# Retention and channel mix on one core: key scaling, key loads, the decay table and the first blocks put in another order

## The chip, the core and the metric

The kernel runs on one core of a Trainium2 chip. TensorE (PE) multiplies matrices, VectorE (DVE) and ScalarE (ACT) work on elements and read TensorE's results from PSUM, GpSimd (POOL) works on elements in SBUF and issues some of the loads, SyncE (SP) issues the others and the stores. Each engine runs its instructions in the order in which they are written; semaphores make one wait for another. The metric is the device time of one execution in microseconds.

## What is computed

A retention layer (linear attention with a decay for each head) whose output goes through a channel mix:

```python
for t in range(S):                                   # B=4, H=8, S=768, D=64
    state = gamma * state + einsum('bhd,bhe->bhde', k[:, :, t], v[:, :, t])
    y[:, :, t] = scale * einsum('bhd,bhde->bhe', q[:, :, t], state)
x = y.transpose(0, 2, 1, 3).reshape(B, S, 512)
x_prev = x shifted by one token, 0 at the start
xk = mu_k * x + (1 - mu_k) * x_prev;  xr = mu_r * x + (1 - mu_r) * x_prev
k = max(xk @ w_k, 0)                                 # 512 -> 1024
out = sigmoid(xr @ w_r) * (k * k @ w_v)              # 1024 -> 512
```

## The kernel before

The 768 tokens of a batch are cut into 6 chunks of 128, so there are 24 chunks (`c`); two chunks make a block of 256 tokens (`m`, 12 of them) for the channel mix.

For a chunk, `load` brings keys as float32 on SP's queue and q and v as float16 on GpSimd's queue. `kscale` (line 108) multiplies the keys by a decay table `gk` and gives `ks`, on GpSimd. `transposes` has TensorE turn q and `ks` (`pT`), and ScalarE copy them (`qkT`). `scores` makes `pA`, masked by VectorE to `a2t`. `state` adds keys times values to the state (`pS`), scaled by VectorE to `sbd`. `retained` makes `pY` from the state and the scores, and VectorE multiplies it by the decay table `gy` into `xT` (line 174).

For a block, `shift` takes the difference `dx` of neighbouring tokens on GpSimd (line 183) and makes four `xk` and four `xr` from it on VectorE (line 188). `keys` is four groups of 8 matmuls (`pZ`), each squared by ScalarE in two operations (`kr`, `k`). `gate` (`pR`, `rsb`) and `values` (`pV`, 8 matmuls for each half) follow a block later, and `store` multiplies them on VectorE (`osb`, line 232) and writes them out.

The order is written by hand. In the loop over `m`, with `a = 2 * (m + 1)`, the scores, states and retained outputs of chunks `a` and `a + 1` alternate with the key groups of block `m`. Then come `shift(m + 1)` and `ahead(a + 2)`, which scales and transposes one chunk, a gate, `ahead(a + 3)`, a gate, and the values of block `m - 1`. So on GpSimd the scaling of a chunk stands behind `dx`, and on TensorE its transposes follow at once. All loaded tiles have five buffers, and the loads of two chunks are written at the top of each turn. `gy` (128 x 512 float32) is loaded from memory.

```python
    ld = pool("ld", 5)
    att = pool("att", 4)
    psa = pool("psa", 4, space=PS)
    psm = pool("psm", 4, space=PS)
```

Of the kernel before, what the change touches and what calls it, by code (L numbers as in the profile page):

```python
# [18 lines left out]
def kernel(  # L19
# [239 lines left out]
    def ahead(c):  # L259
        if c < NC:  # L260
            kscale(c)
            transposes(c)
# [12 lines left out]
    shift(0)
    ahead(2)
    ahead(3)
    for m in range(NBLK + 1):
        a = 2 * (m + 1)
        p = m - 1  # L280
        z = m < NBLK
        if p > 0:
            store(p - 1, 1)
        maybe(load, a + 2)
        maybe(load, a + 3)
        maybe(scores, a)
        maybe(state, a)
        if z:
            keys(m, 0)
        maybe(scores, a + 1)  # L290
# [14 lines left out]
        if p >= 0:
            gate(p, 1)
            values(p, 0)
            store(p, 0)
            values(p, 1)
# [31 lines left out]
```

## Time and profile before

| | us |
|---|---|
| median of 3 runs (227.29 to 228.06) | 227.64 |
| the profiled execution | 227.42 |
| its span, first to last instruction | 225.6 |
| TensorE busy in it (matmuls) | 169.7 |
| VectorE busy | 132.4 |
| ScalarE busy | 98.3 |
| GpSimd busy | 94.5 |

The rows that the prediction uses stand in a section below. In a row of the timeline the first number is the start, the second the time that the row's instructions took together, then come engine, line, operation, the tile written and the tiles read, and how many instructions the row joins; in brackets is how long the engine had been idle and what it waited for. [...] Matmuls are pipelined, so their durations overlap.

### The profile page before, as it was taken

The numbers are of one execution on the slowest core, as the hardware profiler recorded it, in microseconds if no ns is written. First come the engines' busy times: TensorE is split into PE (matmuls) and PEld (weight loads), VectorE is DVE, ScalarE is ACT, GpSimd is POOL, SyncE is SP. The second block draws the span as 40 slices with busy tenths as digits, with TensorE's granted clock in tenths as the row PEclk, the third lists the DMA queues.
The fourth block names the chain that finished last, engine by engine and source line by source line (L and its number), as shares of the span: only waits on it lengthen the run. The fifth ranks groups of instructions, "written<-read, shape, count | busy, mean of one in ns | idle before, by whom it ended". The sixth has DMA issues, their size and how long they took to land.

```text
span 225.6 us, 3597 instructions
## 1 busy us (share of the span) xinstructions
PE 169.7 (75%) x1444; PEld 106.8 (47%) x1444; DVE 132.4 (59%) x220; ACT 98.3 (44%) x146; POOL 94.5 (42%) x92
## 2 busy tenths in 40 slices
PE   0128495877869977986868977986878986999993
PEld 0015264564545564463544464563454464575641
DVE  0007694948747648558747648568748558467022
ACT  2012245566365265165265264166265164163920
POOL 8760845729048039029149029019139025002000
PEclk9999999699996996999996996999996996999999
DMA  7999999954926934943936943942934940100222
GB/s 94 189 194 165 175 198 161 65 35 26 197 62 41 162 79 29 162 93 21 194 67 40 154 88 25 153 100 18 183 82 34 157 92 3 66 27 3 93 93 93
DMA packets 82464, 22.06 MB, mean 98 GB/s; under 512 B 76560, under 2 KB 79248, under 8 KB 82448
## 3 DMA queue, kind: packets, MB, share of 16 engines
q0 software_dynamic: 52544, 8.92, 50.5%
q1 hardware_dynamic: 28848, 12.92, 23.6%
q8 instruction: 11, 0.18, 0.3%
q10 hardware_dynamic: 1056, 0.00, 0.2%
q14 instruction: 5, 0.04, 0.1%
HBM read 24.46 MB, written 6.29 MB: 136 GB/s over the span
## 4 chain that ended last, share of the span: by engine, by line
PE 53%; DVE 16%; issue 11%; POOL 11%; DMA 8%; POOLq 0%; DVEq 0%
PE pV L223 18%; PE pR L213 12%; PE pZ L200 10%; DMA v<-in_v_dram 8%; DVE a2t L132 5%; POOL ks L108 5%; PE pT L117 3%; PE pY L168 3%; DVE osb L232 3%; DVE xT L174 3%; DVE sbd L150 3%; POOL q L102 2%; PE pY L162 2%; PE pS L141 2%; POOL v L104 2%
## 5 line engine op out<-in xcount | busy, mean ns | idle before, releaser
L183 POOL TENSOR_TENSOR dx<-xT 128x1024 f32<-128x1024 f32 x12 | 22.7, 1888 | 106.1 <-DVE xT L174 106.1
L205 ACT ACTIVATE kr<-pZ 128x512 f32<-128x512 f32 x48 | 28.6, 596 | 65.1 <-PE pZ L200 64.9
L188 DVE SCALAR_TENSOR_TENSOR xk<-dx,muk,xT 128x256 f16<-128x256 f32 x48 | 37.1, 832 | 24.7 <-POOL dx L183 24.7
L200 PE MATMUL pZ<-xk,wk 128*128 128x256 f16 x384 | 51.0, 279 | 0.0
L119 ACT COPY qkT<-pT 128x1024 f16<-128x1024 f16 x24 | 24.3, 1013 | 44.2 <-PE pT L117 44.0
L223 PE MATMUL pV<-wv,k 128*128 128x512 f16 x192 | 43.4, 379 | 0.0
L132 DVE TENSOR_TENSOR a2t<-pA,c_sb 128x512 f16<-128x512 f32 x48 | 30.7, 680 | 16.8 <-PE pA L126 16.8
L200 PEld LDWEIGHTS <-wk 128*128 128x128 f16 x384 | 35.7, 100 | 6.2
L117 PE MATMUL pT<-c_sb,ks 128*128 128x128 f16 x96 | 12.5, 270 | 34.7 <-POOL ks L108 34.5
L232 DVE SCALAR_TENSOR_TENSOR osb<-pV,rsb 128x512 f32<-128x512 f32 x24 | 16.5, 691 | 34.8 <-PE pV L223 17.0
L206 ACT ACTIVATE k<-kr 128x512 f16<-128x512 f32 x48 | 30.2, 630 | 1.5
L213 PE MATMUL pR<-wr,xr 128*128 128x512 f16 x96 | 30.6, 456 | 0.0
L223 PEld LDWEIGHTS <-k 128*128 128x128 f16 x192 | 18.8, 98 | 22.7 <-issue 0.2
L108 POOL TENSOR_TENSOR ks<-k,csm_sb 128x512 f16<-128x512 f32 x24 | 26.4, 1119 | 0.1
L117 PEld LDWEIGHTS <-ks 128*128 128x128 f16 x96 | 7.9, 121 | 37.6 <-POOL ks L108 37.6
L174 DVE TENSOR_TENSOR xT<-pY,gy_sb 128x512 f32<-128x512 f32 x24 | 16.6, 691 | 12.9 <-PE pY L168 12.5
L102 POOL DMA_DIRECT2D q<-in_q_dram x24 | 22.3, 928 | 0.8 <-POOLq L325 0.8
L104 POOL DMA_DIRECT2D v<-in_v_dram x24 | 21.6, 898 | 0.4 <-DMA v<-in_v_dram 0.4
L188 DVE SCALAR_TENSOR_TENSOR xr<-dx,mur,xT 128x256 f16<-128x256 f32 x48 | 19.9, 473 | 0.0
L115 PE MATMUL pT<-c_sb,q 128*128 128x128 f16 x96 | 11.7, 258 | 9.9 <-DMA q<-in_q_dram 9.9
L218 ACT ACTIVATE rsb<-pR 128x512 f32<-128x512 f32 x24 | 14.3, 600 | 8.0 <-PE pR L213 7.9
L150 DVE TENSOR_TENSOR sbd<-pS,csm_sb 128x512 f16<-128x512 f32 x24 | 16.3, 680 | 0.0
(22 smaller groups left out, 101.1 us busy)
## 6 DMA issues: line engine op xcount, KB each, us to landing
k<-in_k_dram SPq DMA_DIRECT2D x24, 256.0 KB, 4.0
out_dram<-osb SPq DMA_DIRECT2D x24, 256.0 KB, 2.1
q<-in_q_dram POOLq DMA_DIRECT2D x24, 128.0 KB, 4.0
v<-in_v_dram POOLq DMA_DIRECT2D x24, 128.0 KB, 4.4
wk<-in_moe_w_k_dram POOLq DMA_DIRECT2D x2, 512.0 KB, 12.7
wv<-in_moe_w_v_dram POOLq DMA_DIRECT2D x1, 1024.0 KB, 23.9
wr<-in_moe_w_r_dram POOLq DMA_DIRECT2D x1, 512.0 KB, 19.1
gy_sb<-cgy SPq DMA_DIRECT2D x1, 256.0 KB, 5.4
```

The lines of the kernel that those rows point to most:

```text
L102: nc.gpsimd.dma_start(out=Q16[c], in_=q[b, :, t, :].rearrange("h t d -> t h d"))
L104: nc.gpsimd.dma_start(out=V16[c], in_=v[b, :, t, :].rearrange("h t d -> t h d"))
L108: nc.gpsimd.tensor_tensor(out=KS[c], in0=K32[c], in1=gk[:, :, None].to_broadcast([P, H, D]), op=ALU.mult)
L117: nc.tensor.transpose(pT[:, 1, j, :], KS[c][:, 2 * j : 2 * j + 2, :], ident)
L119: nc.scalar.copy(out=QKT[c], in_=pT)
L132: nc.vector.tensor_tensor(out=A2[c][:, hp], in0=pA[hp], in1=causal[:, None, :].to_broadcast([P, NJ, C]), op=ALU.mult,)
L188: nc.vector.scalar_tensor_tensor(out=dst[:, j], in0=dx[:, j], scalar=mu[:, j : j + 1], in1=xprev[:, j], op0=ALU.mult, op1=ALU.add,)
L200: nc.tensor.matmul(pZ[:, i, :], lhsT=wk16[:, co, fo * P : fo * P + P], rhs=XK[m][:, co, :], start=(i == 0 and co == 0), stop=(co == NCO - ...
L205: nc.scalar.activation(out=kr, in_=pZ, func=AF.Relu)
L206: nc.scalar.activation(out=K2[m][:, 2 * g : 2 * g + 2], in_=kr, func=AF.Square)
L213: nc.tensor.matmul(pR, lhsT=XR[m][:, co, tb * P : tb * P + P], rhs=wr16[:, co, :], start=(co == 0), stop=(co == NCO - 1),)
L223: nc.tensor.matmul(pV, lhsT=K2[m][:, fo, tb * P : tb * P + P], rhs=wv16[:, fo, :], start=(fo == 0), stop=(fo == NFO - 1),)
```

## The change

Five things are changed.

The scaling of keys (`kscale`) can be given an engine. Chunks 0 to 3 are scaled on VectorE, all others on GpSimd as before. In the loop the scaling of chunks `a + 2` and `a + 3` is written at the top of a turn, and their transposes stay at its end, behind `shift(m + 1)`.

Loads of keys are apart from loads of q and v. Keys have a pool of two buffers, and the load of chunk `c + 2` is written behind the scaling of chunk `c`; q and v have eight buffers and are loaded two chunks earlier than before.

The decay table `gy` isn't loaded. VectorE sets its first column and doubles the filled part seven times, with the powers `pw` that are added to the small table `csm`.

The first key load leads SP's queue, ahead of the small tables.

Blocks 0 and 1 are written out by hand: the four key groups of block 0 stand together behind `shift(0)`, and chunks 2 and 3 come after them; the keys of block 1 stand together behind `shift(1)`, followed by both gates of block 0, the transposes of 4 and 5, and the values of block 0 between their scores. The scaling and the transposes of 6 and 7 stand behind `shift(2)`. The loop then runs from `m = 2`.

```diff
-    ld = pool("ld", 5)
+    ld = pool("ld", 8)
+    ldk = pool("ldk", 2)
...
-    def kscale(c):
+    def kscale(c, eng=None):
         KS[c] = att.tile([P, H, D], F16, name="ks16")
-        nc.gpsimd.tensor_tensor(
+        (eng or nc.gpsimd).tensor_tensor(
             out=KS[c], in0=K32[c], in1=gk[:, :, None].to_broadcast([P, H, D]), op=ALU.mult
         )
...
+    loadk(0)
     nc.sync.dma_start(out=csm, in_=smalld.ap())
     nc.sync.dma_start(out=c16, in_=c16d.ap())
+    loadk(1)
...
-    nc.sync.dma_start(out=gy, in_=gyd.ap().rearrange("p (j t) -> p j t", j=NJ))
...
+    nc.vector.memset(gy[:, :, 0:1], 0.125 * KSC)
+    for l in range(LOG):
+        n = 1 << l
+        nc.vector.tensor_tensor(
+            out=gy[:, :, n : 2 * n], in0=gy[:, :, 0:n],
+            in1=pw[:, l, :, None].to_broadcast([P, NJ, n]), op=ALU.mult,
+        )
...
+    for c in (0, 1):
+        kscale(c, nc.vector)
+        loadk(c + 2)
+        transposes(c)
     for c in (0, 1):
         scores(c)
         state(c)
     retained(0)
     retained(1)
     shift(0)
-    ahead(2)
-    ahead(3)
+    for g in range(4):
+        keys(0, g)
+    for c in (2, 3):
+        kscale(c, nc.vector)
+        loadk(c + 2)
+        transposes(c)
...
+    shift(1)
+    kscale(4)
+    loadk(6)
+    kscale(5)
+    loadk(7)
+    for c in range(6, 10):
+        loadqv(c)
+    for g in range(4):
+        keys(1, g)
+    gate(0, 0)
+    gate(0, 1)
+    transposes(4)
+    transposes(5)
+    values(0, 0)
...
+    shift(2)
+    kscale(6)
+    loadk(8)
+    kscale(7)
+    loadk(9)
+    transposes(6)
+    transposes(7)
+    for m in range(2, NBLK + 1):
         a = 2 * (m + 1)
         p = m - 1
         z = m < NBLK
-        if p > 0:
-            store(p - 1, 1)
-        maybe(load, a + 2)
-        maybe(load, a + 3)
+        store(p - 1, 1)
+        for c in (a + 2, a + 3):
+            maybe(kscale, c)
+            maybe(loadk, c + 2)
+        maybe(loadqv, a + 4)
+        maybe(loadqv, a + 5)
...
         maybe(shift, m + 1, NBLK)
-        maybe(ahead, a + 2)
-        if p >= 0:
-            gate(p, 0)
-        maybe(ahead, a + 3)
...
+        maybe(transposes, a + 2)
+        gate(p, 0)
+        maybe(transposes, a + 3)
```

GpSimd around `dx` of block 3 and block 4, before; `ks_773` and `ks_793` are the keys of chunks 8 and 9, whose transposes TensorE has next:

```order
L183 TENSOR_TENSOR dx<-xT_88 128x1024
L108 TENSOR_TENSOR ks_773<-k_635,csm_sb 128x512
L108 TENSOR_TENSOR ks_793<-k_641,csm_sb 128x512
L102 DMA q_839<-in_q_dram 128x8x64
L104 DMA v_841<-in_v_dram 128x8x64
L102 DMA q_845<-in_q_dram 128x8x64
L104 DMA v_847<-in_v_dram 128x8x64
L183 TENSOR_TENSOR dx<-xT_88 128x1024
```

The same place of GpSimd now; `ks_859` and `ks_863` are the keys of chunks 10 and 11, whose transposes stand behind the second `dx` of these rows:

```order
L191 TENSOR_TENSOR dx<-xT_91 128x1024
L116 TENSOR_TENSOR ks_859<-k_659,csm_sb 128x512
L116 TENSOR_TENSOR ks_863<-k_663,csm_sb 128x512
L110 DMA q_867<-in_q_dram 128x8x64
L112 DMA v_869<-in_v_dram 128x8x64
L110 DMA q_871<-in_q_dram 128x8x64
L112 DMA v_873<-in_v_dram 128x8x64
L191 TENSOR_TENSOR dx<-xT_91 128x1024
```

The kinds of rows are the same; the scaling has moved ahead by two chunks.

VectorE at the start of the program, before:

```order
L248 MEMSET xT_87 128x4
L248 MEMSET xT_88 128x4
L248 MEMSET xT_89 128x4
L248 MEMSET xT_90 128x4
L132 TENSOR_TENSOR a2t<-pA_156,c_sb 128x512
L132 TENSOR_TENSOR a2t<-pA_157,c_sb 128x512
```

VectorE at the same place now:

```order
L268 MEMSET gy_sb 128x4
L271 TENSOR_TENSOR gy_sb<-gy_sb,csm_sb 128x4
L271 TENSOR_TENSOR gy_sb<-gy_sb,csm_sb 128x4x2
L271 TENSOR_TENSOR gy_sb<-gy_sb,csm_sb 128x4x4
L271 TENSOR_TENSOR gy_sb<-gy_sb,csm_sb 128x4x8
L271 TENSOR_TENSOR gy_sb<-gy_sb,csm_sb 128x4x16
L271 TENSOR_TENSOR gy_sb<-gy_sb,csm_sb 128x4x32
L271 TENSOR_TENSOR gy_sb<-gy_sb,csm_sb 128x4x64
L116 TENSOR_TENSOR ks_136<-k_96,csm_sb 128x512
L116 TENSOR_TENSOR ks_151<-k_100,csm_sb 128x512
L140 TENSOR_TENSOR a2t<-pA_166,c_sb 128x512
```

The table's eight instructions and two scalings now stand ahead of the first masking of scores.

ScalarE at the start, before; each `COPY` brings one chunk's transposes to SBUF:

```order
L119 COPY qkT<-pT 128x1024 x4
L205 ACTIVATE kr<-pZ 128x512
L206 ACTIVATE k_292<-kr 128x512
L205 ACTIVATE kr<-pZ 128x512
L206 ACTIVATE k_292<-kr 128x512
```

ScalarE at the same place now:

```order
L127 COPY qkT<-pT 128x1024 x2
L213 ACTIVATE kr<-pZ 128x512
L214 ACTIVATE k_243<-kr 128x512
L213 ACTIVATE kr<-pZ 128x512
L214 ACTIVATE k_243<-kr 128x512
L213 ACTIVATE kr<-pZ 128x512
L214 ACTIVATE k_243<-kr 128x512
L213 ACTIVATE kr<-pZ 128x512
L214 ACTIVATE k_243<-kr 128x512
L127 COPY qkT<-pT 128x1024 x2
```

The copies of chunks 2 and 3 have moved behind the eight operations of block 0's keys.

## Rows read from the trace of the kernel before

**Rows 1.** Waits over the span: who waited for whom, us in total, times, longest

```profile
PE pT L117 <- POOL ks L108: 34.5, 12, 7.1
```

**Rows 2.** Timeline of GpSimd, `dx` only: start, duration, instruction, idle time before it

```profile
23.22 1.89 POOL L183 TENSOR_TENSOR dx<-xT 128x1024 f32<-128x1024 f32 x1 [6.86 <-DVE xT L174]
36.21 1.89 POOL L183 TENSOR_TENSOR dx<-xT 128x1024 f32<-128x1024 f32 x1 [5.39 <-DVE xT L174]
49.26 1.89 POOL L183 TENSOR_TENSOR dx<-xT 128x1024 f32<-128x1024 f32 x1 [5.46 <-DVE xT L174]
65.12 1.89 POOL L183 TENSOR_TENSOR dx<-xT 128x1024 f32<-128x1024 f32 x1 [8.27 <-DVE xT L174]
82.86 1.89 POOL L183 TENSOR_TENSOR dx<-xT 128x1024 f32<-128x1024 f32 x1 [10.14 <-DVE xT L174]
100.28 1.89 POOL L183 TENSOR_TENSOR dx<-xT 128x1024 f32<-128x1024 f32 x1 [9.82 <-DVE xT L174]
...
202.53 1.89 POOL L183 TENSOR_TENSOR dx<-xT 128x1024 f32<-128x1024 f32 x1 [13.47 <-DVE xT L174]
```

**Rows 3.** Timeline of GpSimd, TensorE and VectorE in the block behind 82.86

```profile
84.72 2.22 POOL L108 TENSOR_TENSOR ks<-k,csm_sb 128x512 f16<-128x512 f32 x2
84.79 3.23 DVE L188 SCALAR_TENSOR_TENSOR xk<-dx,muk,xT 128x256 f16<-128x256 f32 x4 [2.07 <-POOL dx L183]
85.81 0.61 PE L117 MATMUL pT<-c_sb,ks 128*128 128x128 f16 x4 [2.63 <-POOL ks L108]
87.94 1.67 DVE L188 SCALAR_TENSOR_TENSOR xr<-dx,mur,xT 128x256 f16<-128x256 f32 x4
91.54 0.69 DVE L232 SCALAR_TENSOR_TENSOR osb<-pV,rsb 128x512 f32<-128x512 f32 x1 [1.94 <-issue]
93.27 0.69 DVE L232 SCALAR_TENSOR_TENSOR osb<-pV,rsb 128x512 f32<-128x512 f32 x1 [1.03 <-PE pV L223]
93.88 1.28 DVE L132 TENSOR_TENSOR a2t<-pA,c_sb 128x512 f16<-128x512 f32 x2
```

**Rows 4.** Busy time of PE, PEld, DVE, ACT and POOL in one block, PEclk, DMA

```profile
82.80:100.30 17.50, 14.31 (x126) 9.11 (x124) 11.17 (x18) 8.03 (x12) 7.62 (x8) 0.90 0.71 91
```

**Rows 5.** Granted clock (third number from the end) of two stretches; key groups at either clock

```profile
58.00:62.00 4.00, 3.22 (x42) 2.41 (x41) 3.67 (x7) 1.23 (x2) 0.00 (x0) 1.00 1.43 232
68.20:71.40 3.20, 3.20 (x17) 1.85 (x16) 3.20 (x8) 1.74 (x3) 3.20 (x4) 0.50 0.19 12
...
32.23 1.04 PE L200 MATMUL pZ<-xk,wk 128*128 128x256 f16 x8
41.95 1.91 PE L200 MATMUL pZ<-xk,wk 128*128 128x256 f16 x8
```

**Rows 6.** Timeline of TensorE in a block without the low clock

```profile
103.22 0.40 PE L117 MATMUL pT<-c_sb,ks 128*128 128x128 f16 x4 [2.63 <-POOL ks L108]
...
109.18 0.40 PE L126 MATMUL pA<-qkT 64*128 64x128 f16 x8
...
116.07 0.39 PE L115 MATMUL pT<-c_sb,q 128*128 128x128 f16 x4
```

**Rows 7.** Timeline of VectorE: the last four `xk`, with no `ks` beside them

```profile
204.46 1.67 DVE L188 SCALAR_TENSOR_TENSOR xk<-dx,muk,xT 128x256 f16<-128x256 f32 x4 [2.07 <-POOL dx L183]
```

**Rows 8.** Start: one key and one query load (KB, us to landing); GpSimd's timeline

```profile
k<-in_k_dram SPq DMA_DIRECT2D x1, 256.0 KB, 4.9
q<-in_q_dram POOLq DMA_DIRECT2D x1, 128.0 KB, 8.0
...
3.18 0.89 POOL L102 DMA_DIRECT2D q<-in_q_dram  x1
14.31 2.04 POOL L108 TENSOR_TENSOR ks<-k,csm_sb 128x512 f16<-128x512 f32 x2
```

**Rows 9.** The page's groups: count, busy us, mean ns of one, idle before

```profile
L205 ACT ACTIVATE kr<-pZ 128x512 f32<-128x512 f32 x48 | 28.6, 596 | 65.1 <-PE pZ L200 64.9
L206 ACT ACTIVATE k<-kr 128x512 f16<-128x512 f32 x48 | 30.2, 630 | 1.5
```

More of the change, by code (lines that the diff above doesn't have):

```diff
@@ L44 @@
     COLS = S + 1
+    LOG = 7
     NC = B * NCH
@@ L53 @@
     h_pj = 2 * np.arange(NJ)[None, :] + (np.arange(P) // D)[:, None]
-    gy_np = (0.125 * KSC) * gam[h_pj][:, :, None] ** ar[None, None, :]
+    pw_np = gam[h_pj][:, None, :] ** (2.0 ** np.arange(LOG)[None, :, None])
     half = (np.arange(2)[None, :] == (np.arange(P) // D)[:, None]).astype(np.float64)
     gs_np = (gam[h_pj] ** C)[:, :, None] * half[:, None, :]
-    small_np = np.concatenate([gk_np, gs_np.reshape(P, -1)], axis=1).astype(np.float32)
+    small_np = np.concatenate(
+        [gk_np, gs_np.reshape(P, -1), pw_np.reshape(P, -1)], axis=1
+    ).astype(np.float32)
     c16d = nc.inline_tensor(c16_np, name="c16")
     smalld = nc.inline_tensor(small_np, name="csmall")
-    gyd = nc.inline_tensor(gy_np.astype(np.float32).reshape(P, -1), name="cgy")
     def pool(name, bufs, **kw):
@@ L75 @@
     c16 = const.tile([P, 2 * P], F16, name="c16_sb")
-    csm = const.tile([P, H + 2 * NJ], F32, name="csm_sb")
+    csm = const.tile([P, H + 2 * NJ + LOG * NJ], F32, name="csm_sb")
     gy = const.tile([P, NJ, C], F32, name="gy_sb")
@@ L86 @@
     gk = csm[:, 0:H]
-    gs = csm[:, H:].rearrange("p (j h) -> p j h", j=NJ)
+    gs = csm[:, H : H + 2 * NJ].rearrange("p (j h) -> p j h", j=NJ)
+    pw = csm[:, H + 2 * NJ :].rearrange("p (l j) -> p l j", l=LOG)
     ctx.enter_context(tc.manual_schedule())
@@ L93, with loadk, loadqv @@
     PV = {}
-    def load(c):
+    def loadk(c):
         b, ci = divmod(c, NCH)
         t = slice(ci * C, ci * C + C)
-        K32[c] = ld.tile([P, H, D], F32, name="k32")
+        K32[c] = ldk.tile([P, H, D], F32, name="k32")
         nc.sync.dma_start(out=K32[c], in_=k[b, :, t, :].rearrange("h t d -> t h d"))
+    def loadqv(c):
+        b, ci = divmod(c, NCH)
+        t = slice(ci * C, ci * C + C)
         Q16[c] = ld.tile([P, H, D], F16, name="q16")
@@ L237, in store @@
         nc.sync.dma_start(out=out[b, s0 : s0 + P, :], in_=osb)
+    loadk(0)
     nc.sync.dma_start(out=csm, in_=smalld.ap())
     nc.sync.dma_start(out=c16, in_=c16d.ap())
+    loadk(1)
     nc.scalar.dma_start(out=muk, in_=moe_mu_k.rearrange("(co ci) -> ci co", ci=P))
     nc.scalar.dma_start(out=mur, in_=moe_mu_r.rearrange("(co ci) -> ci co", ci=P))
-    load(0)
-    nc.sync.dma_start(out=gy, in_=gyd.ap().rearrange("p (j t) -> p j t", j=NJ))
-    load(1)
-    for b in range(B):
-        nc.vector.memset(xT[b][:, :, 0:1], 0.0)
     wks = moe_w_k.rearrange("(co ci) f -> ci co f", ci=P)
     wvs = moe_w_v.rearrange("(fo fi) e -> fi fo e", fi=P)
+    loadqv(0)
+    loadqv(1)
     for h in range(2):
@@ L253 @@
         nc.gpsimd.dma_start(out=wk16[:, :, f], in_=wks[:, :, f])
-    load(2)
-    load(3)
+    loadqv(2)
+    loadqv(3)
     nc.gpsimd.dma_start(out=wr16, in_=moe_w_r.rearrange("(co ci) e -> ci co e", ci=P))
     nc.gpsimd.dma_start(out=wv16, in_=wvs)
[L259 to L262, printed above, removed]
+    for b in range(B):
+        nc.vector.memset(xT[b][:, :, 0:1], 0.0)
+    nc.vector.memset(gy[:, :, 0:1], 0.125 * KSC)
[5 more added lines that the diff above has]
+        )
     def maybe(fn, c, n=NC):
@@ L266, in maybe @@
             fn(c)
-    ahead(0)
-    ahead(1)
+    for c in (0, 1):
+        kscale(c, nc.vector)
+        loadk(c + 2)
+        transposes(c)
     for c in (0, 1):
@@ L275 @@
     shift(0)
-    ahead(2)
-    ahead(3)
-    for m in range(NBLK + 1):
+    for g in range(4):
[4 more added lines that the diff above has]
+        transposes(c)
+    loadqv(4)
+    loadqv(5)
+    for c in (2, 3):
+        scores(c)
+        state(c)
+    retained(2)
+    retained(3)
+    shift(1)
[12 more added lines that the diff above has]
+    values(0, 0)
+    store(0, 0)
+    scores(4)
+    state(4)
+    values(0, 1)
+    scores(5)
+    state(5)
+    retained(4)
+    retained(5)
+    shift(2)
[6 more added lines that the diff above has]
+    for m in range(2, NBLK + 1):
         a = 2 * (m + 1)
@@ L300 @@
         maybe(shift, m + 1, NBLK)
-        maybe(ahead, a + 2)
-        if p >= 0:
-            gate(p, 0)
-        maybe(ahead, a + 3)
[L305 to L309, printed above, removed]
+        maybe(transposes, a + 2)
+        gate(p, 0)
+        maybe(transposes, a + 3)
+        gate(p, 1)
+        values(p, 0)
+        store(p, 0)
+        values(p, 1)
     store(NBLK - 1, 1)
```

## The prediction

> **What bounds the kernel now.** I read the list of waits first: TensorE's largest stall is at the transposes of the scaled keys (`pT` from `ks`), which wait for GpSimd's `ks`, 34.5 us in 12 waits [rows 1]. Then the starts of `dx`, one for each block of 256 tokens, which divide the span: dx0 at 23.22, dx1 at 36.21, dx2 at 49.26, dx3 at 65.12, dx4 at 82.86 and dx11 at 202.53 [rows 2]. From dx3 to dx11 eight blocks take 137.41 us, 17.2 each; behind dx11 come 23.1 us to the end of the span.
>
> The block from dx4 to dx5 shows the cause, read in order of time [rows 2, 3]. `dx` at 82.86 waits for `xT`. GpSimd then does two `ks`, and TensorE stands 2.63 us until the first of them is done (85.81). Gate and values stand behind that, so `osb` on VectorE waits 1.94 and 1.03 us, although VectorE was through with `xk` and `xr` at 89.61. In 17.50 us TensorE works 14.31 and VectorE 11.17: neither is full, each waits for the other [rows 4]. Moreover the granted clock is 0.50 from 68.2 to 71.4, behind such a stand, and 1.00 from 58 to 62, ahead of it [rows 5]: transposes, gate and values then begin at 1.2 GHz instead of 2.4.
>
> **The loop after the change.** On GpSimd two `ks` still follow dx3, but they are now those of chunks 10 and 11 instead of 8 and 9, and their transposes stand one block later, behind the next `xT`. The stand of 2.63 us goes, and with it the low clock behind it. What is late next?
>
> TensorE: in a block without the low clock it took 5.96 us from the transposes of `ks` (103.22) to the next `pA` (109.18) [rows 6]. With 0.39 for the transposes of `q` ahead of it, the next `pA` can start some 6.4 us after `dx`, and both `pV` are done by then.
> VectorE, by starts after dx4 at 82.86 [rows 2, 3]: `xk` +1.93, `xr` +5.08, behind it (1.67 less 0.05 overlap) +6.70, two `osb` of some 0.63 each without their waits, `a2t` at +7.95; from `a2t` at 93.88 to the next `dx` at 100.28 it is another 6.40. Sum 14.35 us.
> VectorE is there 1.6 us after TensorE, so it sets the block: the loop xT, dx, xk, xr, osb, a2t, sbd, xT, 14.35 us. TensorE alone would need 6.4 + 6.89 (109.18 to 116.07, [rows 6]) = 13.3. A block that opens a batch has no earlier state to add; I take 0.25 off, 14.1.
>
> The contention inside the loop stays. Four `xk` take 3.23 us beside `ks` and 1.67 alone [rows 3, 7], and `ks` still follows `dx` directly. Only the last block ahead of dx11 has no `ks` left: 14.35 - 1.56 = 12.8, but TensorE's work is near that, so 13.0.
> From dx3 to dx11: 5 x 14.35 + 2 x 14.1 + 13.0 = 113.0 us instead of 137.4, a gain of 24.4. If TensorE alone set it (13.3) it would be 106, and with half a microsecond more in each block, where an engine takes over from another, 117.
>
> The key loads now wait for one of two buffers. A load is issued on SP's queue behind a store, whose `osb` ends some 8 us after `dx`, and once the `ks` two chunks earlier is done; its own `ks` comes 8 us later still. A load took 4.9 us in the crowd of the start [rows 8], so it is hidden. On GpSimd four loads of q and v (used a block later) and the next `dx` are queued behind a late `ks`; the `dx` would be late from some 6 us of further lateness on. The q and v loads have eight buffers and run further ahead: nothing. After the last block nothing changes: 23.1 us.
>
> **The start** is put in another order, so each stage is summed apart.
> To dx0, 23.22 before. GpSimd's `ks` started at 14.31, behind its queue of DMA issues [rows 8]. Now VectorE scales. The first key load leads its queue: flight 4.9, landed at 5 to 6. The table: seven products of 4 to 256 elements a partition, each between nothing and the 0.42 us of an `xr` of 256 elements, 0 to 2.9 in all; since small ones must have a fixed part, 1.8. One scaling on VectorE lies between that 0.42 and GpSimd's 1.11; nearest is `a2t` with as many elements, 0.64 [rows 3]. So the first `ks` is ready near 8, and q of chunk 1 is late next: issued at 3.18, flight 8.0, 11.2 [rows 8]. Before, the second `ks` ended at 16.35 and dx0 came 6.87 later; 11.2 + 6.87 = 18.1, a little less as fewer key loads and no table compete: 17.8. Gain 5.4.
> dx0 to dx1, 13.0 before. Keys of block 0 now stand whole between the two pairs of chunks. 1.9 for dx and 0.4 for the first xk; four groups of 8 matmuls, 1.04 us each at 2.4 GHz and 1.91 at 1.2 [rows 5]; behind the first of them (1.7) ScalarE needs two operations of 0.6 for each group, 4.9 in all [rows 9], and the copies of the next scores are queued behind these, 1.0 to the first. From there to `dx` the stretch of 6.4. Sum 16.3. Loss 3.3.
> dx1 to dx2, 13.05 before. dx 1.9, four xk beside ks 3.2, the rest of the keys of block 1 between 3.5 and 6.1 by the clock, 4.6; gate, transposes and values 6.4; of the stretch from scores to `dx` what is not beside these, 4.5. Sum 20.6. Loss 7.5. Gate and values of block 0 lie in it, which stood ahead of dx3 before.
> dx2 to dx3, 15.86 before. Here `ks` of chunks 6 and 7 still stand between `dx` and their transposes, so one stand remains beside VectorE's 14.1: 14.5. Gain 1.4.
> dx3 thus at 17.8 + 16.3 + 20.6 + 14.5 = 69.2 instead of 65.12: the start as a whole loses 4.1. Bounds: 65 (keys at the fast clock, copies hidden) and 75 (the low clock in every key group, each copy late).
>
> **Sum.** 69.2 + 113.0 + 23.1 = 205.3 us of span. The profiled execution took 227.42 with a span of 225.6, so 1.8 lie around it: 207.1. It stands within 0.1% of the median of the runs, 227.64. Forecast 207 us.
>
> **Rivals.** (1) TensorE's clock falls in the waits that are left. In the new loop TensorE spends its lead of 1.6 us in two stands, about half each, ahead of the second `pA` and the second `pS`, for VectorE. If it falls there, two key groups, a `pS` and two `pY` run at 1.2 GHz, and these lie on the loop: twice 1.91 - 1.04 [rows 5], and as much again half over for the smaller ones, 2.7 us a block. Against it: the beginning of a block (58 to 62), with shorter waits at the same places, kept 1.00, and the fall came behind a stand of 2.63. For it: two stands close together with little work between. In three or four blocks it gives 215 to 218; in all eight 207 + 8 x 2.7 = 229, slower than before. It turns the sign from about seven and a half blocks on.
> [...]
> (2) `ks` slips behind `xk`, because its key load lands late. Then `xk` takes 1.67 and TensorE's 13.3 set the loop: some 7 less, 196 to 200. Against it: the margin of the load, above.
> [...]
> (3) TensorE is not freed: the transposes still wait for `ks`, since the gated load comes too late. With the loss of the start that is 227 + 4 = 231. It takes loads some 15 us long.
> (4) The start alone is worse than summed, dx3 at 75: 213.
>
> **How the numbers follow.** The loop on VectorE as summed, 201 to 213: 0.66, (4) at its upper end. Clock low in part, 213 to 222: 0.14. Clock low in nearly all blocks, 222 to 229: 0.06, half of it without gain. (2): 0.09. (3): 0.03. Anything else: 0.02. To leave out no more than 0.2 the range is 199 to 219. Faster by over 0.3% (what a measurement of this kernel can tell from no change): 0.91; within 0.3%: 0.02; slower: 0.07.
>
> **What would show it.** Right: no wait of the key transposes for `ks` behind dx3; starts of `dx` 14.1 to 14.4 apart from dx3 on, the granted clock at 1.00 there; `osb` without idle time ahead of it; four `xk` still at 3.2; dx0 near 18, dx3 near 69. Wrong: `dx` 16 to 17 apart with the clock at 0.50 behind the second scores; `ks` waiting for a key load; dx3 beyond 75 or under 65.

## The result and the profile after

The changed kernel takes 207.59 us (median of 4 runs, 207.46 to 207.88) against 227.85 for the kernel before in the same comparison: a ratio of 0.910, interval 0.905 to 0.915. The profiled execution took 207.57 with a span of 205.8. The forecast was 207.

First the starts of `dx` on GpSimd, to be laid beside [rows 2] (start, duration, instruction, idle time before it).

```profile
16.30 1.89 POOL L191 TENSOR_TENSOR dx<-xT 128x1024 f32<-128x1024 f32 x1 [4.73 <-DVE xT L182]
33.18 1.89 POOL L191 TENSOR_TENSOR dx<-xT 128x1024 f32<-128x1024 f32 x1 [11.48 <-DVE xT L182]
54.50 1.89 POOL L191 TENSOR_TENSOR dx<-xT 128x1024 f32<-128x1024 f32 x1 [10.22 <-DVE xT L182]
70.21 1.89 POOL L191 TENSOR_TENSOR dx<-xT 128x1024 f32<-128x1024 f32 x1 [3.73 <-DVE xT L182]
84.40 1.89 POOL L191 TENSOR_TENSOR dx<-xT 128x1024 f32<-128x1024 f32 x1 [6.59 <-DVE xT L182]
...
182.73 1.89 POOL L191 TENSOR_TENSOR dx<-xT 128x1024 f32<-128x1024 f32 x1 [11.39 <-DVE xT L182]
```

From dx3 to dx11 it is 112.52 us instead of 137.41, a gain of 24.9. dx3 comes at 70.21 instead of 65.12, a loss of 5.1. The end behind dx11 is 23.07, as before. 24.9 - 5.1 = 19.8 is the whole difference of the spans (225.6 and 205.8).

The block from dx4 to dx5 in order of time, TensorE, VectorE and GpSimd, as in [rows 3]:

```profile
84.62 0.39 PE L125 MATMUL pT<-c_sb,ks 128*128 128x128 f16 x4
86.25 2.22 POOL L116 TENSOR_TENSOR ks<-k,csm_sb 128x512 f16<-128x512 f32 x2
86.32 3.23 DVE L196 SCALAR_TENSOR_TENSOR xk<-dx,muk,xT 128x256 f16<-128x256 f32 x4 [2.01 <-POOL dx L191]
88.42 0.96 POOL L110 DMA_DIRECT2D q<-in_q_dram  x1
89.47 1.66 DVE L196 SCALAR_TENSOR_TENSOR xr<-dx,mur,xT 128x256 f16<-128x256 f32 x4
91.05 1.28 DVE L240 SCALAR_TENSOR_TENSOR osb<-pV,rsb 128x512 f32<-128x512 f32 x2
92.25 1.28 DVE L140 TENSOR_TENSOR a2t<-pA,c_sb 128x512 f16<-128x512 f32 x2
92.98 0.38 PE L134 MATMUL pA<-qkT 64*128 64x128 f16 x7 [0.44 <-DVE a2t L140]
94.18 0.38 PE L149 MATMUL pS<-sbd,c_sb 128*128 128x512 f16 x1 [0.82 <-DVE sbd L158]
```

The transposes `pT` of the scaled keys follow at once, with no bracket behind them. `osb` has none either: VectorE runs from `xk` to the masks without a pause, and TensorE stands twice for VectorE, 0.44 and 0.82 us. The four `xk` still take 3.23 beside the two `ks`.

The same block as a window (busy time of PE, PEld, DVE, ACT and POOL, PEclk, DMA), to compare with [rows 4]; then the page's row of TensorE's granted clock in 40 slices of the span (PEclk; a window gives it as a share of full speed, this row in tenths, with 9 for 0.90 or more); then two lines of the list of waits.

```profile
84.40:98.65 14.25, 12.99 (x126) 8.47 (x124) 10.98 (x18) 7.71 (x12) 7.61 (x7) 1.00 0.86 113
```

```profile
PEclk9999998599968899999999999999999999999999
```

```profile
PE pZ L208 <- DVE xk L196: 8.5, 3, 4.4
...
PE pT L125 <- POOL ks L116: 4.7, 2, 4.1
```

TensorE did 14.31 us in the block before and does 12.99 now, with the same 126 matmuls: what is gone is the time at the low clock (PEclk 0.90 before, 1.00 now). In the row of the granted clock that now shows only ahead of dx3 (slices 7, 8 and 12 to 14, of 5.1 us each). The first matmuls of the span, to some 24 us, take the longer times too (four transposes 0.61 us, as against 0.39 in the rows above), though the row has 9 there. The wait for `ks`, 34.5 us in 12 waits before [rows 1], is 4.7 in two, both in the block from dx2 to dx3. The three waits for `xk`, 8.5 us, are part of the price of the new start: they stand ahead of the key groups of blocks 0 and 1, which now follow `dx` directly.

### The profile page after: what moved, and what is told of

Its sections match the earlier page's. It is cut to its first block, busy times and chain, and to the rows that moved or that the text cites. A ratio compares the mean times of both kernels' runs of the same rounds, so it can differ in the third digit from the quotient of the medians.

```text
span 205.8 us, 3572 instructions
## 1 busy us (share of the span) xinstructions
PE 164.2 (80%) x1444; PEld 104.3 (51%) x1444; DVE 132.7 (64%) x232; ACT 95.2 (46%) x146; POOL 90.4 (44%) x88
## 4 chain that ended last, share of the span: by engine, by line
PE 55%; DVE 25%; issue 7%; POOL 5%; ACT 3%; DMA 3%; POOLq 0%; DVEq 0%
PE pZ L208 17%; PE pV L231 15%; PE pR L221 9%; DVE a2t L140 6%; DVE xr L196 6%; DVE osb L240 5%; PE pY L176 4%; DVE sbd L158 3%; DMA q<-in_q_dram 3%; POOL dx L191 3%; DVE xk L196 3%; PE pS L149 2%; PE pT L123 2%; PE pT L125 2%; PE pY L170 2%
## 5 line engine op out<-in xcount | busy, mean ns | idle before, releaser
L208 PE MATMUL pZ<-xk,wk 128*128 128x256 f16 x384 | 55.4, 294 | 8.6 <-DVE xk L196 8.5
L196 DVE SCALAR_TENSOR_TENSOR xk<-dx,muk,xT 128x256 f16<-128x256 f32 x48 | 34.1, 768 | 24.6 <-POOL dx L191 24.6
L208 PEld LDWEIGHTS <-wk 128*128 128x128 f16 x384 | 37.9, 104 | 18.5 <-issue 10.5
L240 DVE SCALAR_TENSOR_TENSOR osb<-pV,rsb 128x512 f32<-128x512 f32 x24 | 15.7, 682 | 18.8 <-PE pV L231 12.4
L221 PE MATMUL pR<-wr,xr 128*128 128x512 f16 x96 | 24.0, 379 | 0.0
L116 POOL TENSOR_TENSOR ks<-k,csm_sb 128x512 f16<-128x512 f32 x20 | 22.3, 1131 | 2.0 <-PE pS L153 1.8
L196 DVE SCALAR_TENSOR_TENSOR xr<-dx,mur,xT 128x256 f16<-128x256 f32 x48 | 20.7, 491 | 0.0
L134 PE MATMUL pA<-qkT 64*128 64x128 f16 x192 | 12.2, 229 | 7.6 <-DVE a2t L140 5.1
L158 DVE TENSOR_TENSOR sbd<-pS,csm_sb 128x512 f16<-128x512 f32 x24 | 16.3, 679 | 0.0
L123 PE MATMUL pT<-c_sb,q 128*128 128x128 f16 x96 | 9.7, 226 | 8.2 <-DMA q<-in_q_dram 8.2
L134 PEld LDWEIGHTS <-qkT 64*128 64x128 f16 x192 | 6.5, 98 | 16.2 <-issue 12.5
```

The lines of the kernel that those rows point to most:

```text
L158: nc.vector.tensor_tensor(out=SBD[c].rearrange("p j (h d) -> p j h d", h=2), in0=pS.rearrange("p j (h d) -> p j h d", h=2), in1=gs[:, :, : ...
L196: nc.vector.scalar_tensor_tensor(out=dst[:, j], in0=dx[:, j], scalar=mu[:, j : j + 1], in1=xprev[:, j], op0=ALU.mult, op1=ALU.add,)
L208: nc.tensor.matmul(pZ[:, i, :], lhsT=wk16[:, co, fo * P : fo * P + P], rhs=XK[m][:, co, :], start=(i == 0 and co == 0), stop=(co == NCO - ...
L221: nc.tensor.matmul(pR, lhsT=XR[m][:, co, tb * P : tb * P + P], rhs=wr16[:, co, :], start=(co == 0), stop=(co == NCO - 1),)
L240: nc.vector.scalar_tensor_tensor(out=osb, in0=PV.pop((m, tb)), scalar=1.0 / (KSC * KSC), in1=RS.pop((m, tb)), op0=ALU.mult, op1=ALU.mult,)
```

## The experiments

Each run is compared with the kernel before on the same chip; since that one's median lay between 227.9 and 229.7, ratios and spans say more than times. The lines quoted are those of each kernel's own trace, and diffs are against the changed kernel.

### What sets the loop

**The order on GpSimd undone in the loop.**

```diff
@@ top of the turn
-        for c in (a + 2, a + 3):
-            maybe(kscale, c)
-            maybe(loadk, c + 2)
@@ behind maybe(shift, m + 1, NBLK)
+        for c in (a + 2, a + 3):
+            maybe(kscale, c)
+            maybe(loadk, c + 2)
```

> The changed kernel with one part undone: in the loop the scaling of the two keys and the two key loads stand again behind the subtraction of dx, right before the transposes that read them; the start and everything else stay. Theory (the gain is the loop, freed of TensorE's wait for ks): the wait of pT for ks comes back in each block, eight blocks from dx3 to dx11 cost again about 137 us instead of 112.5, the time is 70.2 + 137.4 + 23.1 + 1.8 = 232.5, range 228 to 235. Rival (the gain is in the scaling on VectorE, the gated loads or the table, not in the order on GpSimd): 207 to 209.

Measured: 229.61 us, ratio 1.002 (0.998 to 1.006), 135.7 us from dx3 to dx11. The whole gain is gone, and the wait is back (first line: one block; second: the list of waits):

```profile
87.61 0.61 PE L125 MATMUL pT<-c_sb,ks 128*128 128x128 f16 x4 [2.63 <-POOL ks L116]
```

```profile
PE pT L125 <- POOL ks L116: 25.2, 10, 4.1
```

So without these three lines in their place the other parts of the change give nothing in the loop. Nor does the loop need those parts: with keys 0 to 3 on GpSimd, with five key buffers, with the table loaded, and with the old start (runs below), the eight blocks take 112.5 to 112.6 us as well. The earlier loads of q and v were not undone alone; but behind dx3 TensorE waits for no load of q or v in the trace before or after.

**More work on TensorE.** In `gate`, for half 0 of blocks 1 to 11:

```diff
-        for co in range(NCO):
-            nc.tensor.matmul(pR, ...)
+        for _ in range(2 if tb == 0 and m > 0 else 1):
+            for co in range(NCO):
+                nc.tensor.matmul(pR, ...)
```

> The changed kernel with the four gate matmuls of the first half of a block run twice (the second run overwrites the first), for eleven blocks: 0.86 to 1.03 us more of TensorE in each. Theory (VectorE sets the loop): the second osb and the mask have room for it, the loop stays at 14.2 to 14.4, only the tail's one or two blocks show it, 208.5 to 210.5. Rival (TensorE sets the loop): 11 x 0.86 to 1.03 more, 217 to 219.

Measured: 211.10 us, ratio 0.920 (0.914 to 0.925), span 209.3. The first seven blocks behind dx3 take 14.19, 14.25, 14.03, 14.25, 14.25, 14.03 and 14.25 us, in no place over 0.01 from those without the added work. Nearly all of the cost is at the end: the last block before dx11 takes 14.13 instead of 13.28, and the tail 25.6 instead of 23.1. The time is 0.6 us above the range: at the end the added work stands on TensorE's own chain four times, once in the last block and three times in the tail, not in one or two blocks. In the last block TensorE has no room and the addition costs 0.85; in the seven others it costs nothing. The window shows the room that TensorE had there (columns as above; the added work is in the second number):

```profile
84.50:98.75 14.25, 13.65 (x130) 8.77 (x128) 10.98 (x18) 7.81 (x12) 7.61 (x8) 1.00 0.85 113
```

**More work on VectorE.**

```diff
         maybe(loadqv, a + 5)
+        if z:
+            nc.vector.tensor_tensor(
+                out=junk, in0=gy, in1=causal[:, None, :].to_broadcast([P, NJ, C]), op=ALU.mult)
         maybe(scores, a)
```

> The changed kernel with one more operation on VectorE in each of ten loop turns, between xr and the mask of the scores: 128x512, out of and into the state memory, its result unused; by xT and a2t of the same size 0.5 to 0.7 us. Theory (VectorE sets the loop): every block is longer by that operation, 10 x 0.5 to 0.7, the time 212.5 to 215. Rival A (TensorE sets it, VectorE has room): 207.5 to 208.5. Rival B (TensorE's clock falls once its waits in a block grow from 1.3 to 1.9 us): pZ x8 1.9 instead of 1.04 in many blocks, granted clock at half for stretches, 220 or more.

Measured: 220.23 us, ratio 0.960 (0.953 to 0.966), span 218.7: above the theory's range, because the theory and rival B are both true. Against the changed kernel the eight blocks behind dx3 are longer by 0.60, 2.16, 2.16, 0.61, 2.15, 2.11, 0.61 and 0.60 us. 0.6 is the added operation (0.67 in its row, less overlap), as it must be if VectorE sets the loop. Alone this would not show it: the operation stands between `osb` and the mask, and the last block, which TensorE sets, is longer by 0.60 too. It takes the run before this to exclude TensorE. The other 1.5 is in four blocks, those in which the clock fell (granted clock 0.89 to 0.90, 1.00 in the four others). Two blocks that differ in that alone, and the first of them in order of time:

```profile
86.91:103.32 16.41, 14.55 (x126) 9.36 (x124) 11.58 (x19) 7.71 (x12) 7.61 (x7) 0.90 0.74 98
...
119.51:134.37 14.86, 12.94 (x125) 8.41 (x124) 11.58 (x19) 7.71 (x12) 7.60 (x8) 1.00 0.82 107
```

```profile
94.77 0.67 DVE L344 TENSOR_TENSOR junk<-gy_sb,c_sb 128x512 f16<-128x512 f32 x1
...
96.09 0.38 PE L135 MATMUL pA<-qkT 64*128 64x128 f16 x7 [1.04 <-DVE a2t L141]
...
97.29 0.48 PE L150 MATMUL pS<-sbd,c_sb 128*128 128x512 f16 x1 [0.81 <-DVE sbd L159]
...
97.99 1.91 PE L209 MATMUL pZ<-xk,wk 128*128 128x256 f16 x8
```

The first stand grew from 0.44 to 1.04 us, and behind the second the key group takes 1.91 us instead of 1.04, as at the low clock in [rows 5]. But the length of the stands does not decide it alone. The block at 119.51 kept the clock with a first stand that is a little longer, and a second of 0.82:

```profile
128.70 0.38 PE L135 MATMUL pA<-qkT 64*128 64x128 f16 x7 [1.11 <-DVE a2t L141]
```

The changed kernel thus stands at most 0.6 us of VectorE from losing the clock in every second block; what picks the blocks is open.

### The four xk beside ks

**The scaling behind the loads.**

```diff
-        for c in (a + 2, a + 3):
-            maybe(kscale, c)
-            maybe(loadk, c + 2)
         maybe(loadqv, a + 4)
         maybe(loadqv, a + 5)
+        for c in (a + 2, a + 3):
+            maybe(kscale, c)
+            maybe(loadk, c + 2)
```

> The changed kernel with the two scalings of the loop written behind the four value and query loads instead of ahead of them. Theory (VectorE sets the loop, and its four xk take 3.23 us instead of 1.66 only because the two ks run beside them): four load issues of 0.9 us put ks 3.6 us later, beside xr and osb; xk x4 falls to about 1.7, the waits of pA for a2t and of pS for sbd go, the loop goes from 14.2 to TensorE's own 13.0 to 13.3, the time is 207.6 - 8 x 1.0 = 199.6, range 198 to 202. Rival A (xk is not on the path of the loop, or TensorE bounds it at 14.2): 207 to 208. Rival B (the overlap only moves, xr takes 3.2 instead of xk): VectorE's sum is the same, 206.5 to 208.5, with xr long.

Measured: 226.06 us, ratio 0.983 (0.977 to 0.990). None of the three was right: nearly all of the gain is lost. Timeline of VectorE and GpSimd in one block, single instructions, and TensorE behind them:

```profile
90.34 0.96 POOL L110 DMA_DIRECT2D q<-in_q_dram  x1
90.44 0.48 DVE L196 SCALAR_TENSOR_TENSOR xk<-dx,muk,xT 128x256 f16<-128x256 f32 x1 [2.01 <-POOL dx L191]
90.84 1.27 DVE L196 SCALAR_TENSOR_TENSOR xk<-dx,muk,xT 128x256 f16<-128x256 f32 x1
...
92.03 1.26 DVE L196 SCALAR_TENSOR_TENSOR xk<-dx,muk,xT 128x256 f16<-128x256 f32 x1
93.61 3.27 DVE L196 SCALAR_TENSOR_TENSOR xr<-dx,mur,xT 128x256 f16<-128x256 f32 x4
93.92 2.27 POOL L116 TENSOR_TENSOR ks<-k,csm_sb 128x512 f16<-128x512 f32 x2
...
98.72 0.38 PE L134 MATMUL pA<-qkT 64*128 64x128 f16 x7 [2.06 <-DVE a2t L140]
```

`xr` now lies beside `ks` and takes 3.27, as rival B has it. But `xk` takes 3.25 as well, with only the issue of loads beside it. VectorE's chain is 1.6 us longer instead of shorter, TensorE's stand is 2.06, and the clock falls in each of the six blocks that have such loads (granted clock 0.90): these are longer by 2.9 to 3.2 us, 1.6 for `xr` and 1.5 for the clock, the price found in the run before this.

**The scaling held back until the state is updated.** Two buffers for `ks` instead of four; the loads at the top of the turn, and:

```diff
         maybe(state, a)
+        maybe(kscale, a + 2)
+        maybe(loadk, a + 4)
...
         maybe(state, a + 1)
+        maybe(kscale, a + 3)
+        maybe(loadk, a + 5)
```

> The changed kernel with two instead of four buffers for the scaled keys, and in the loop each scaling written behind the state update that frees its buffer: so the two ks of a block run beside the masks and the state updates (which read the accumulators), behind the value and query loads, and not beside xk or xr. The run with ks behind the loads showed xr x4 3.27 beside ks, and xk x4 3.25 beside nothing but the issue of the loads. Theory A (issuing loads on GpSimd right behind dx holds up xk by itself): xk x4 stays near 3.25, xr 1.66, the loop stays near 14.2, 206 to 209. Theory B (it was the ks queued directly behind the loads that held up both): xk and xr 1.67 each, the loop goes to TensorE's 13.0 to 13.3, 198 to 201. Rival (the ks are now late for the transposes): a wait of pT for ks, blocks over 14.5, clock falls, 212 or more.

Measured: 200.28 us, ratio 0.881 (0.876 to 0.887). Theory B. One block:

```profile
84.49 0.96 POOL L111 DMA_DIRECT2D q<-in_q_dram  x1
84.58 1.67 DVE L197 SCALAR_TENSOR_TENSOR xk<-dx,muk,xT 128x256 f16<-128x256 f32 x4 [2.01 <-POOL dx L192]
...
86.17 1.67 DVE L197 SCALAR_TENSOR_TENSOR xr<-dx,mur,xT 128x256 f16<-128x256 f32 x4
...
89.60 1.28 DVE L141 TENSOR_TENSOR a2t<-pA,c_sb 128x512 f16<-128x512 f32 x2
...
89.91 1.04 POOL L117 TENSOR_TENSOR ks<-k,csm_sb 128x512 f16<-128x512 f32 x1 [1.83 <-PE pS L154]
...
91.53 0.38 PE L150 MATMUL pS<-sbd,c_sb 128*128 128x512 f16 x1 [0.56 <-DVE sbd L159]
```

The same loads stand right behind `dx`, and `xk` and `xr` take 1.67 each. `ks` runs beside `a2t`, which reads the accumulator: it takes 1.04 us, and the two `a2t` 1.28, as in the changed kernel's block, where no `ks` is beside them. The loop goes to 13.28 us (13.05 where a batch opens), 105.8 for eight blocks.

**No scaling on GpSimd in the loop.**

```diff
+    def kscale_act(c):
+        KS[c] = att.tile([P, H, D], F16, name="ks16")
+        for h in range(H):
+            nc.scalar.activation(out=KS[c][:, h], in_=K32[c][:, h],
+                                 func=AF.Copy, scale=gk[:, h : h + 1])
...
-            maybe(kscale, c)
+            maybe(kscale_act, c)
```

> The changed kernel with the loop's keys scaled on ScalarE, eight operations of 128x64 for a chunk, written where GpSimd's scaling stood: GpSimd does only dx and the issue of loads. By kr (596 ns for 512 columns) and the copy of qkT (990 ns for 1024) 64 columns take about 0.26 us, 16 of them 4.2 us, against a gap of 3.8 us on ScalarE ahead of the first kr. Theory A (the issue of loads right behind dx holds up xk): xk x4 3.25, 206 to 209. Theory B (only ks on GpSimd does): xk x4 1.67, loop 13.0 to 13.5, 198 to 202. Rival (ScalarE becomes late for kr and the loop goes by it): 205 to 215.

Measured: 199.14 us, ratio 0.875 (0.870 to 0.881): Theory B again, 13.28 us a block. Sixteen operations of ScalarE took 3.92 us, a little less than estimated:

```profile
84.13 1.67 DVE L203 SCALAR_TENSOR_TENSOR xk<-dx,muk,xT 128x256 f16<-128x256 f32 x4 [2.07 <-POOL dx L198]
...
86.27 3.92 ACT L123 ACTIVATE ks<-k,csm_sb 128x64 f16<-128x64 f32 x16
```

Two ways of taking `ks` off `xk` end at the same 13.28: what is left is TensorE's work and one stand of 0.56 us for `sbd` (12.72 + 0.56). The other 0.97 us of the changed kernel's 14.25 were those `xk`.

### The start

**Keys 0 to 3 scaled on GpSimd.**

```diff
-        kscale(c, nc.vector)
+        kscale(c)
```

> The changed kernel with the scaling of keys 0 to 3 on GpSimd again, in the same places of the order; the loop and the loads stay. Theory: the first two ks stand behind GpSimd's twelve load issues, which end at 11.6, and take 1.1 us each, so ks1 is ready at 13.9 instead of 8.2, dx0 comes at 20.5 to 21.5 instead of 16.3; the next blocks take up part of it, since keys wait there for weights; dx3 72 to 75, time 209 to 213. Rival (the start is bounded by the landing of loads): 207 to 208.5.

Measured: 212.21 us, ratio 0.933 (0.927 to 0.940); dx0 at 20.64 (4.3 later), dx3 at 74.26 (4.1 later). All three lie in their ranges, but the next blocks take back only 0.3 us. The first transposes of scaled keys wait for GpSimd behind its loads:

```profile
12.85 0.61 PE L125 MATMUL pT<-c_sb,ks 128*128 128x128 f16 x4 [4.48 <-POOL ks L116]
```

**Five buffers for the keys.** `ldk = pool("ldk", 5)` instead of 2. (The gate of the next text is the wait of a key load for a free buffer.)

> The changed kernel with five buffers for the keys instead of two, so that key loads 2, 3 and 4 no longer wait for a scaling. Theory (the gate keeps 768 KB out of the way of the first queries, values and weights): dx0 17.5 to 20, time 208.5 to 211; the loop, whose key loads have time, stays at 112.5 for eight blocks. Rival (the gate does nothing): 207 to 208.

Measured: 210.53 us, ratio 0.917 (0.910 to 0.925), span 207.4 instead of 205.8. The interval overlaps that of the changed kernel, so the ratio alone is no verdict; the traces show where time is lost. dx0 is at 17.53, 1.2 later, and dx3 at 71.81, 1.6 later: the query of chunk 1 comes 1.2 us later behind the extra key loads (first row of this run, second of the changed kernel). The loop is the same, 112.5.

```profile
10.47 0.61 PE L123 MATMUL pT<-c_sb,q 128*128 128x128 f16 x4 [2.12 <-DMA q<-in_q_dram]
```

```profile
9.24 0.61 PE L123 MATMUL pT<-c_sb,q 128*128 128x128 f16 x4 [0.89 <-DMA q<-in_q_dram]
```

**The table loaded.** The eight operations that build `gy` are out, and `nc.sync.dma_start(out=gy, ...)` stands ahead of `loadk(1)`.

> The changed kernel with the decay table loaded from memory again (256 KB ahead of key 1) instead of doubled on VectorE. Theory (the start moves about 160 to 190 GB/s, every load behind it comes later by 1.4 us, VectorE saves 1.85 us that stand ahead of ks0): dx0 16.3 + 0.5 to 1.4, the time 208 to 209.2. Rival (VectorE's chain is what counts): dx0 earlier, 206 to 207.5.

Measured: 208.22 us, ratio 0.905 (0.897 to 0.912), which overlaps that of the changed kernel. dx0 is 0.5 later, dx3 0.6 earlier (in the block ahead of it one key group took 1.91 us, where in the changed kernel three took 1.64 to 1.79). No verdict: doubling the table on the chip is worth 0.5 us at dx0 and nothing that can be told at the end.

**The old start with the new loop.** Load order, table, scaling on GpSimd and the order of the first blocks are those of the kernel before, with four buffers for the keys; the loop is that of the changed kernel:

```diff
+    for m in range(NBLK + 1):
...
+        if m < 2:
+            maybe(loadqv, a + 2)
+            maybe(loadqv, a + 3)
+        for c in (a + 2, a + 3):
+            maybe(kscale, c)
+            maybe(loadk, c + 2)
+        if m > 0:
+            maybe(loadqv, a + 4)
+            maybe(loadqv, a + 5)
```

> The start of the kernel before (its load order, the decay table loaded, four keys scaled on GpSimd, one block after the other from the first turn on) with the loop of the changed kernel (keys scaled and loaded two chunks ahead; value and query loads ahead from the second turn on). Theory (the new start costs more at dx3 than it gains at dx0): dx0 23.2, then 13.0, 13.1 and 14.2 for the next three blocks, dx3 63.5 instead of 70.2, time 63.5 + 112.5 + 23.1 + 1.8 = 200.9, range 199.5 to 204. Rival (the new start pays: the old one with the new loop is as late or later): 207 to 212.

Measured: 205.17 us (203.6 to 209.0), ratio 0.899 (0.892 to 0.906), just above the range; dx at 24.05, 37.82, 54.07 and 68.10. dx3 is 2.1 us earlier than in the changed kernel, not 6.7: the block from dx1 to dx2 took 16.25. Its query of chunk 5 is issued behind `wv`; TensorE waited 3.44 us, and the key group behind that took 1.92 us, in a stretch (40.7 to 50.9) for which the page has a granted clock of 0.5:

```profile
42.29 0.61 PE L125 MATMUL pT<-c_sb,q 128*128 128x128 f16 x4 [3.44 <-DMA q<-in_q_dram]
...
44.63 1.92 PE L210 MATMUL pZ<-xk,wk 128*128 128x256 f16 x8
```

**The first blocks in the loop's order.** Keys 0 to 3 and the later loop stay as in the changed kernel; the scaling of keys 4 and 5 and the loads of keys 6 and 7 come ahead of `shift(1)`:

```diff
     shift(0)
-    for g in range(4):
-        keys(0, g)
+    keys(0, 0)
+    keys(0, 1)
...
+    for c in (4, 5):
+        kscale(c)
+        loadk(c + 2)
+    keys(0, 2)
     for c in (2, 3):
         scores(c)
         state(c)
+    keys(0, 3)
     retained(2)
     retained(3)
     shift(1)
...
-    for m in range(2, NBLK + 1):
+    for m in range(1, NBLK + 1):
```

> The changed kernel with its first blocks ordered as the loop orders the others: keys of block 0 in between the scores and states of chunks 2 and 3, and block 1 by the loop's own turn; loads, scaling of keys 0 to 3 and the later loop stay. Theory (setting the first blocks apart costs TensorE time there: dx0 to dx1 16.9, dx1 to dx2 21.3): dx0 stays at 16.3, dx1 comes near 30.8, dx2 at 45 to 48 (the values and queries 4 and 5 land behind wv, 31.5 to 34.5), dx3 59 to 63, the time 59 to 63 + 112.5 + 23.1 + 1.8 = 196.5 to 200.5. Rival (the first blocks are bounded by the landing of the loads, the order hides it): 205 to 208.

Measured: 201.85 us, ratio 0.880 (0.874 to 0.886), dx at 16.94, 35.67, 50.50 and 64.53. dx3 is 5.7 us earlier, so setting the first blocks apart does cost that much, and the rival falls. But the time is above the expected 196.5 to 200.5. dx1 came at 35.67 instead of 30.8: its `xT` was ready at 31.6, but on GpSimd it stood behind the scaling of key 5, which waited for its load, and that load had had to wait for a free buffer.

```profile
34.67 1.04 POOL L116 TENSOR_TENSOR ks<-k,csm_sb 128x512 f16<-128x512 f32 x1 [1.44 <-DMA k<-in_k_dram]
35.67 1.89 POOL L191 TENSOR_TENSOR dx<-xT 128x1024 f32<-128x1024 f32 x1
```

### All together

```diff
-    for h in range(2): ... wk ...
-    loadqv(2); loadqv(3)
-    ... wr ...; ... wv ...
+    loadqv(2); loadqv(3)
+    for h in range(2): ... wk ...
+    loadqv(4); loadqv(5)
+    ... wr ...; ... wv ...
...
+    kscale_act(2)
+    kscale_act(3)
...
+    for m in range(NBLK + 1):
```

> A version from what the runs have shown: the changed kernel with (1) the keys from chunk 2 on scaled on ScalarE, (2) the first blocks ordered as the loop's, (3) queries and values 2 to 5 loaded ahead of the weights that come later (2 and 3 ahead of wk, 4 and 5 ahead of wr and wv). Expected: dx0 16.5, dx1 26.5 to 30, dx2 40 to 43, dx3 53 to 57, then 105.8 for eight blocks, 23.1 and 1.8: 184 to 188. Rival (the start is bounded by the landing of loads or by the clock at half): dx3 60 or more, 191 or more.

Measured: 191.90 us, ratio 0.834 (0.827 to 0.841): the fastest kernel here, 8% below the changed one by the two ratios (0.834 / 0.910 = 0.917). The time is above the expected 184 to 188. The loop is as expected, 106.1. The start is the rival's: dx at 17.97, 30.30, 47.58 and 60.66. From dx1 to dx2 it took 17.28, since ScalarE, and TensorE behind it, waited for the load of key 5. With two buffers it could be issued only when key 3 was scaled, at 20.46 (first row), and it took 12.9 us to land, where the median key load of this run takes 4.2:

```profile
20.46 0.37 SPq L108 DMA_DIRECT2D k<-in_k_dram  x1
...
33.48 2.02 ACT L127 ACTIVATE ks<-k,csm_sb 128x64 f16<-128x64 f32 x8 [4.46 <-DMA k<-in_k_dram]
...
34.12 0.29 PE L137 MATMUL pT<-c_sb,ks 128*128 128x128 f16 x1 [2.98 <-ACT ks L127]
```

With that block at 13.3 the time would be some 188, by estimate. A third buffer, or loads two chunks earlier, was not tried.

## Why the prediction was right, and where it was not

| term | predicted | measured |
|---|---|---|
| start to dx0 | 17.8 | 16.30 |
| dx0 to dx1 | 16.3 | 16.88 |
| dx1 to dx2 | 20.6 | 21.32 |
| dx2 to dx3 | 14.5 | 15.71 |
| dx3 to dx11 | 113.0 | 112.52 |
| behind dx11 | 23.1 | 23.07 |
| around the span | 1.8 | 1.8 |

**The loop** was right in its mechanism and its size: 14.25 us in a plain block (14.35 predicted), 14.03 where a batch opens (14.1). That VectorE sets it and TensorE has room is shown by the runs together: 0.66 us more of TensorE (13.65 against 12.99) lengthens the seven blocks by nothing, 0.67 us on VectorE by 0.6, and 1.56 us less in the four `xk` shortens a plain block by 0.97, down to TensorE's time. The last block, 13.0 predicted, took 13.28. For it the prediction took "TensorE's work is near that, so 13.0", under its own 13.3 for TensorE alone; 13.3 was right, since the plain blocks of the two runs without `ks` beside `xk` take 13.28 too.

**dx0** was 1.5 us too late, by one term. The table (1.85, predicted 1.8) and the scaling (0.68, predicted 0.64) came as summed (the fixed part of a small product was an estimate that no row before showed; the shortest of the seven took 0.17 us), but the query of chunk 1, for which the next transposes wait, landed at 9.24 instead of 11.2. I had taken the flight of [rows 8] from a start in which the old table and more keys competed, and allowed 0.3 us for their absence; it was 2. The run with five key buffers (landing at 10.47) shows 1.2 of that for the keys. From there to dx0 it was 7.1 (6.87 used).

**dx0 to dx3** was 2.5 us too early in all, half of it from dx2 to dx3. There `ks` still stood between `dx` and its transposes, as the prediction said. But I had put that stand beside VectorE's work and at the full clock. TensorE waited 4.09 us, and the first three key groups behind that took 1.77, 1.79 and 1.64 us, at a granted clock of 0.58, 0.53 and 0.62. The clock accounts for the error: in the run with the table loaded the same wait of 4.09 stood there, only the first key group behind it was slow (1.91, the next 1.04), and the block took 14.16. The two errors of the start cancel but for 1.0 us: the forecast of dx3 (69.2) is closer than its parts, and that 207 came within 0.6 of the measured time is in part luck.

**Rival 1**, the clock in the waits that are left, did not come in the loop, but it was nearer than its 0.14 + 0.06 say. In the changed kernel a first stand of 0.44 to 0.73 us and a second of 0.82 kept the clock in seven blocks behind dx3, and the last block has a single stand of 0.56. With the added work on VectorE a first stand of 1.04 to 1.32 lost it in four of seven, with the scaling behind the loads one of 2.04 to 2.35 in six of six; the second stayed 0.82. Its price was too high: 1.5 us a block where I had worked out 2.7 (one key group of 1.91 us in the rows above, not two), so that all eight blocks would have given some 220 and not a loss. But a loop whose clock falls anew at each turn is what the run with the scaling behind the loads shows: the granted clock is 0.90 in each of its six blocks. No run shows a clock in GHz: where the prediction has 2.4 and 1.2 GHz, the traces have a granted clock of 1.00 and 0.50, as in the kernel before beside the two key groups of [rows 5] (1.04 us at 32.23, 1.91 at 41.95).

**Rival 2** had its price right, 196 to 200: taking `ks` off `xk` gives 199.1 and 200.3. But its way, `ks` slipping behind `xk` by a late load, would perhaps not have given it: where `ks` merely stood behind other work on GpSimd and was ready, both `xk` and `xr` were held up (3.25 and 3.27 us). **Rival 3** did not come: the only waits for `ks` are those ahead of dx3. **Rival 4** is what scaling on GpSimd would have brought (212.2).

## What to carry to other kernels

Scaling two chunks one turn earlier on GpSimd was worth 23 us in eight blocks (135.7 against 112.5), because TensorE and VectorE waited for each other across it: look for the short wait at which the chains of two engines meet, and move what releases it a turn ahead. Look for operations of two engines that take longer side by side: here four `xk` on VectorE took 3.23 us beside two `ks` on GpSimd and 1.67 without, while two `a2t`, which read the accumulators, took 1.28 with or without `ks`. Moving `ks` from the one to the other gave 0.97 us in a plain block. This tuned loop stands just short of the low clock: 0.6 us more on VectorE cost 2.1 to 2.2 in four of eight blocks.

## What the runs showed of the hardware

**In the rows below, an `xk` that meets a `ks` ends behind it.** Single rows of the changed kernel: of the four `xk` two meet a `ks` and take 1.25 and 1.26 us, the other two 0.47 and 0.48. The two end 0.28 us behind the `ks` that each meets (87.28 and 88.47). So each is longer by 0.78 us, less than the 1.03 and 1.22 of those `ks`. Whether such an operation stood for a part of that time or ran slowly through all of it, no run separates.

```profile
86.32 1.25 DVE L196 SCALAR_TENSOR_TENSOR xk<-dx,muk,xT 128x256 f16<-128x256 f32 x1 [2.01 <-POOL dx L191]
87.49 1.26 DVE L196 SCALAR_TENSOR_TENSOR xk<-dx,muk,xT 128x256 f16<-128x256 f32 x1
88.68 0.47 DVE L196 SCALAR_TENSOR_TENSOR xk<-dx,muk,xT 128x256 f16<-128x256 f32 x1
```

**A ready `ks` queued behind the issue of loads on GpSimd held up VectorE twice**: once ahead of its own row, beside the loads (four `xk` 3.25 us), and once beside its row (four `xr` 3.27). Loads alone (0.9 us each) did not: `xk` took 1.67 with loads and no `ks` behind them, and 1.67 with loads and a `ks` that still waited for a buffer. What happens in between was not settled.

**In the last kernel loads held up GpSimd's queue.** Its 24th load waited 3.16 us for the landing of the one eight places ahead, `wv`, and so did others for theirs (`wv` itself 1.01); there this delayed dx0, which stood behind `wv`'s own issue (17.97, though its `xT` was ready at 16.2). Whether the chip or the program's semaphores make these loads wait, the rows do not say.

```profile
16.99 0.88 POOL L278 DMA_DIRECT2D wv<-in_moe_w_v_dram  x1 [1.01 <-DMA v<-in_v_dram]
...
37.97 0.88 POOL L116 DMA_DIRECT2D v<-in_v_dram  x1 [3.16 <-DMA wv<-in_moe_w_v_dram]
```
